# Attention and two expert layers in one kernel: weights read in 1 MB pieces, one subtraction on VectorE, zero rows written near head 12

## The chip, the cores and the metric

The kernel runs on one core of a Trainium2 chip. The metric is the time of one execution on the device in microseconds (us), the median of several runs. Engines are named as in the profile: PE is TensorE's matmul, PEld its loading of weights, DVE is VectorE, ACT ScalarE, POOL GpSimd and SP SyncE, which here issues nearly all DMA transfers.

## What is computed

Everything is float32. Cut to what matters:

```python
# q, k, v: 4 batches x 8 heads x 576 x 64; block-causal mask, blocks of 64
attn = softmax(q @ k.T / 8 + mask) @ v                 # 32 heads
x = attn.transpose(0, 2, 1, 3).reshape(2304, 512)
h = (x @ w1) * (x @ w2)                                # 512 -> 1024
x = (h @ w3) @ w_out                                   # 1024 -> 1024 -> 512
noisy = x @ w_gate + log1p(exp(x @ w_noise)) * noise   # 8 experts
top2, weights = two largest of noisy, softmax over the two
out[t] = sum over the two experts e: weight * (relu(x[t] @ e_w1[e]) @ e_w2[e])
```

## The kernel before

The work is staged in three. **Attention** goes over 32 heads. **MoE1** computes the dense expert and the router in nine chunks (`CH` = 256 tokens) and fills PE's gaps between heads. The **expert phase** (`phase3`) follows, eight experts on gathered rows. Two slots per token go into a table `idt` in DRAM, the rows themselves into `yt`.

Precision comes from pairs: a float32 value is split into a high part (a rounded copy, made by ACT) and a low part (value less high part), and `mm3` multiplies with three matmuls (lines 485 to 487). `split` (line 476 on ACT, line 480 on DVE) makes such a pair.

The dense weights `w1`, `w2`, `w3`, `w_out` lie in DRAM as 64-bit floats. They come in 40 pieces of 512 KB (`w_jobs`); `load64` (line 538) has SP load one into a tile `stg`, of which there are two; `conv64` (lines 547 to 549) makes float32 of it on DVE with three integer instructions, writing a tile `stf` (also two), and `split` then writes the pair into its resident tile `pc`. The load of piece n + 2 is issued behind the conversion of piece n, which sets its `stg` free. One call of `feed` does the `split` of the piece converted last and the conversion of the next. Some pieces may not be converted before a count of matmul units has been issued.

The order of the work is written out by hand in two strings of steps for each head, `FIRST` for heads up to 9 and `LATER` behind them: `s0`..`s3` are the scores of the next head (`s_unit`, lines 639 to 642) with their row maxima on DVE (line 653) and exponentials on ACT (line 658); `g0`..`g3` transpose the probabilities on PE (line 672) and copy them to `pt` (line 676); `a`, `b0`, `b1` multiply by v (lines 685, 697); `h` prepares the head after (`prep_h`, lines 607 to 612); `c` calls `feed`; `f2.9` asks for 2.9 us of fill. The fill is first 64 units (192 matmuls of 128x512) that fold `w3` and `w_out` into one matrix (`w_unit`), then MoE1's chunks: `ab` (lines 485 to 487, 128x256, three to a product) needs `w1` and `w2` pieces. A scheduler then orders each engine's queue by priorities; an engine works through its queue in order.

`prep_h` splits q and k: ACT makes both high parts `hi`, DVE the low part of q in place, POOL the low part of k, `kl` (line 612). POOL has little else to do among the first eight heads.

`setup` fills two small tiles `tr0`, `tr1`, and `setup_dram(0)` (lines 133 to 148) writes the empty-slot entries into `idt` (runs of 12, 8 and 512 bytes) and zeroes the last rows of `yt`, 0.8 MB. It is called at head 4 of the written order, and the scheduler puts it far ahead of that. The first slots are scattered into `idt` at 260.8 us.

## Time and profile before

| | |
|---|---|
| median of 3 runs | 1100.47 us (1100.3 to 1101.81) |
| profiled execution, its own time | 1103.1 us |
| its span, first to last instruction | 1101.2 us |
| mean granted clock of TensorE | 0.988 of full speed |
| busy over the span: PE, PEld | 1050.4 us, 941.2 us |
| busy over the span: DVE, ACT, POOL | 564.4 us, 494.9 us, 309.3 us |
| DMA | 136.34 MB, 124 GB/s in the mean |

The profile is of one execution on the chip. Busy time is the time in which an engine had at least one instruction at work; matmuls overlap, and their ends are modelled. A line such as "DVE stf L547 <- DMA stg" is read as: the instruction of line 547 that writes `stf` on DVE waited for the transfer into `stg`. The chain is the row of waits and work that ended last, followed backwards.

### The profile page before, as it was taken

Reading aid. Unit: us, or ns where it says so; the run is one execution under the profiler, and the core shown is the slowest. Engines: PE = TensorE matmul, PEld = TensorE weight load, DVE = VectorE, ACT = ScalarE, POOL = GpSimd, SP = SyncE. Lnnn points to the kernel's source line nnn. Section 1 sums busy time; section 2 is a strip of 40 time slices with the busy share of each in tenths; the row PEclk is TensorE's granted clock in tenths of the full one; section 3 lists DMA queues with packets and bytes.
Section 4 is the critical chain, followed back from the end, with each engine's and each line's share of the span. In section 5 each row is a group of like instructions: output and inputs, shape, how many; then the busy total and the mean of one; then the engine's idle time right before and its main releaser. Section 6 shows DMA issues by size and latency. Waiting matters only on the chain.

```text
span 1101.2 us, 17515 instructions
## 1 busy us (share of the span) xinstructions
PE 1050.4 (95%) x6588; PEld 941.2 (85%) x6588; DVE 564.4 (51%) x1270; ACT 494.9 (45%) x1180; POOL 309.3 (28%) x315
## 2 busy tenths in 40 slices
PE   4999978999999999999999999999999999999996
PEld 3767767799899999989999889889898989899885
DVE  5988889856665756532454453534333333434111
ACT  5765547666665656422223432433333333333111
POOL 3110122424252242422443325241413222120211
PEclk9999989999999999999999999999999999999999
DMA  9765775325634463322413556563545445351212
GB/s 218 237 199 193 196 200 180 123 79 132 196 96 105 143 156 121 107 68 59 77 40 87 126 106 184 173 163 96 148 102 144 107 125 125 106 115 30 39 20 32
DMA packets 80386, 136.34 MB, mean 124 GB/s; under 512 B 21437, under 2 KB 46757, under 8 KB 80293
## 3 DMA queue, kind: packets, MB, share of 16 engines
q1 hardware_dynamic: 70181, 113.98, 36.4%
q0 software_dynamic: 10112, 21.16, 10.7%
q8 instruction: 54, 0.88, 0.3%
q14 instruction: 39, 0.32, 0.1%
HBM read 103.92 MB, written 31.19 MB: 123 GB/s over the span
## 4 chain that ended last, share of the span: by engine, by line
PE 81%; DMA 8%; DVE 7%; ACT 1%; issue 1%; SPq 1%; POOL 0%; POOLq 0%; DVEq 0%; ACTq 0%
PE ph L485 13%; PE ph L486 13%; PE ph L487 13%; PE m L485 9%; PE m L486 9%; PE m L487 9%; DMA stg<-in_w_dram 4%; PE tp L672 4%; PE av L697 3%; PE sb L642 2%; PE sb L639 2%; PE m L939 1%; DVE stf L549 1%; DVE nm L653 1%; DMA stf<-in_m_dram 1%
## 5 line engine op out<-in xcount | busy, mean ns | idle before, releaser
L485 PE MATMUL m<-xh,pc 128*128 128x256 f32 x576 | 165.2, 290 | 5.6 <-DVE at L211 3.5
L486 PE MATMUL m<-xh,pc 128*128 128x256 f32 x576 | 163.1, 287 | 2.2 <-DVE xh L480 2.2
L487 PE MATMUL m<-xh,pc 128*128 128x256 f32 x576 | 161.2, 287 | 1.9 <-DVE pc L480 1.9
L485 PE MATMUL ph<-xt,pc 128*128 128x384 f32 (+1 forms) x512 | 156.0, 308 | 2.9 <-ACT xt L476 1.6
L486 PE MATMUL ph<-xt,pc 128*128 128x384 f32 (+1 forms) x512 | 157.0, 307 | 0.0
L487 PE MATMUL ph<-xt,pc 128*128 128x384 f32 (+1 forms) x512 | 156.9, 307 | 0.0
L954 DVE SCALAR_TENSOR_TENSOR ht<-ph,ht 128x384 fp32r<-128x384 f32 (+1 forms) x128 | 61.6, 489 | 148.7 <-ACT ht L953 143.5
L480 DVE TENSOR_TENSOR pc<-stf,pc 128x1024 fp32r<-128x1024 f32 (+1 forms) x92 | 92.3, 1016 | 87.2 <-ACT pc L476 83.8
L485 PE MATMUL ph<-pc,ht 128*128 128x512 f32 x320 | 127.8, 400 | 0.0
L486 PE MATMUL ph<-pc,ht 128*128 128x512 f32 x320 | 126.5, 396 | 0.0
L487 PE MATMUL ph<-pc,ht 128*128 128x512 f32 x320 | 126.4, 395 | 0.0
L981 POOL DMA_INDIRECT out_dram<-yo,ids x40 | 64.3, 1606 | 211.5 <-ACT yo L977 124.0
L485 PEld LDWEIGHTS m<-xh,pc 128*128 128x128 f32 x576 | 110.5, 193 | 7.2 <-DVE at L211 3.7
L953 ACT ACTIVATE ht<-ph 128x384 fp32r<-128x384 f32 (+1 forms) x128 | 55.0, 437 | 133.8 <-PE ph L487 127.1
L486 PEld LDWEIGHTS m<-xh,pc 128*128 128x128 f32 x576 | 110.3, 193 | 3.0 <-DVE xh L480 2.6
L487 PEld LDWEIGHTS m<-xh,pc 128*128 128x128 f32 x576 | 109.0, 192 | 2.7 <-DVE pc L480 2.4
L476 ACT CAST pc<-stf 128x1024 fp32r<-128x1024 f32 (+1 forms) x92 | 78.1, 864 | 73.8 <-DVE stf L549 32.5
L658 ACT ACTIVATE pb<-sb,nm 128x288 f32<-128x288 f32 (+3 forms) x192 | 93.5, 496 | 38.4 <-PE tp L672 17.3
L480 POOL TENSOR_TENSOR gt<-at,gt 128x256 fp32r<-128x256 f32 x72 | 57.2, 798 | 183.9 <-ACT gt L476 175.7
L485 PEld LDWEIGHTS ph<-xt,pc 128*128 128x128 f32 x512 | 95.7, 188 | 4.0 <-ACT xt L476 2.1
L612 POOL TENSOR_TENSOR kl<-qk,hi 128x576 fp32r<-128x576 f32 x32 | 47.5, 1484 | 177.2 <-ACT hi L610 136.6
L486 PEld LDWEIGHTS ph<-xt,pc 128*128 128x128 f32 x512 | 96.2, 188 | 0.6 <-DVE xt L480 0.2
(158 smaller groups left out, 2229.0 us busy)
## 6 DMA issues: line engine op xcount, KB each, us to landing
stf<-in_m_dram SPq DMA_DIRECT2D x52, 512.0 KB
...
```

The lines of the kernel that those rows point to most:

```text
L476: d = nc.scalar.copy(h, src)
L480: return d, eng.tensor_tensor(l, src, r32(h), op=OP.subtract)
L485: nc.tensor.matmul(out, a, c, start=first, stop=False)
L486: nc.tensor.matmul(out, a, d, start=False, stop=False)
L487: nc.tensor.matmul(out, b, c, start=False, stop=last)
L612: nc.gpsimd.tensor_tensor(c.kl, c.qk[:, 1, :], r32(c.hi[:, 1, :]), op=OP.subtract)
L658: nc.scalar.activation(pb[t][:, k0:k0 + src.free_size()], src, AF.Exp, bias=nm, scale=1.0, accum_out=sums[:, h // H, t + n, h % H:h % H + 1])
L672: nc.tensor.transpose(bank[:, n * P:(n + 1) * P], pb[t][:, kt * P:(kt + 1) * P], self.ident)
L697: nc.tensor.matmul(c.av[:, o0:o0 + w], c.vv[:, kt, :], c.pt[:, i, s0:s0 + w], start=(kt == 0 and i == 0), stop=(kt == 4 and i == m - 1))
L953: a = nc.scalar.activation(hh[:, 0, f, :], ph, AF.Relu)
L954: v = nc.vector.scalar_tensor_tensor(hh[:, 1, f, :], ph, 0.0, r32(hh[:, 0, f, :]), op0=OP.max, op1=OP.subtract)
L981: nc.gpsimd.indirect_dma_start(out=self.a["out"], out_offset=self.idx(e, i), in_=yo, in_offset=None, compute_op=OP.add)
```

## The change

- **Pieces.** `w_jobs` now gives 23 pieces for the same bytes: six of 512 KB among the first nine, and 17 of 1 MB. `stg` tiles are 8 KB a partition (two), `stf` is one tile of 4 KB instead of two of 2 KB. `moe1.conv` still counts half pieces.
- **Steps.** `FIRST` calls `feed` three times a head instead of five.
- **kl.** For heads 0 to 8 DVE makes `kl`, not POOL.
- **Table and zero rows.** `setup_dram(0)` is called at head 12, issued behind the store of head 11's result. `tr0` lies in one of the three `y` tiles until then.
- **Memory.** `pt` of heads 0 to 7 lies where `pt` of the later heads will; `stg` and `stf` get their own pool, closed at the last piece, and `yT` lies in a pool that opens then; tiles of the expert phase get padding and other names (not shown).

```diff
@@ -67,7 +67,7 @@
 
 
 
-FIRST = "g0 g1 t f2.9 c t c o g2 g3 t p s0 t t s1 s2 f2.9 c t a f2.9 t b0 t s3 h t t c c b1 v l"
+FIRST = "g0 g1 t f2.9 c t o g2 g3 t p s0 t t s1 s2 f2.9 c t a f2.9 t b0 t s3 h t t c b1 v l"
 LATER = "g0 g1 f2.6 o g2 p t c g3 t t t s0 s1 s2 t c t a f2.6 s3 b0 t t c f2.6 c t b1 h v l"
 
 
@@ -116,7 +117,7 @@
         self.wcat = p2.tile([P, 4, P], F32R, name="wcat")
         nc.scalar.copy(self.wcat, wg)
         nc.gpsimd.tensor_tensor(self.wcat[:, :, 16:32], wg[:, :, 0:16], r32(self.wcat[:, :, 0:16]), op=OP.subtract)
-        self.tr0 = self.px.tile([P, E, NSLOT], I32, name="tr0")
+        self.tr0 = p2.tile([P, 512], I32, name="y", bufs=3)[:, 0:E * NSLOT].rearrange("p (e s) -> p e s", e=E)
         nc.gpsimd.iota(self.tr0, pattern=[[0, E], [0, NSLOT]], base=NT, channel_multiplier=1)
         self.tr1 = p2.tile([NOV, P], I32, name="lt")
         nc.gpsimd.iota(self.tr1, pattern=[[1, P]], base=NT, channel_multiplier=0)
@@ -534,7 +535,8 @@
         return [(tab[:, b * P:e * P].rearrange("e (p i) -> p e i", p=P), ids[:, :, b:e]) for b, e in ((0, NA), (NA, NSLOT))]
 
     def load64(self, src, n):
-        t = self.stg.tile([P, 512], I64, name="stg")
+        w = n * src.shape[-1]
+        t = self.stg.tile([P, 1024], I64, name="stg", bufs=2)[:, 0:w]
         self.nc.sync.dma_start(t.rearrange("p (a b) -> p a b", a=n), src)
         return t
 
@@ -542,7 +544,7 @@
 
         v = self.nc.vector
         wi = t.bitcast(I32).rearrange("p (n w) -> p n w", w=2)
-        f = self.stg.tile([P, 512], F32, name="stf")
+        f = self.stg.tile([P, 1024], F32, name="stf")[:, 0:wi.shape[1]]
         fi = f.bitcast(I32)
         v.tensor_scalar(fi, wi[:, :, 1], 0x07FFFFFF, 3, op0=OP.bitwise_and, op1=OP.logical_shift_left)
         v.scalar_tensor_tensor(fi, wi[:, :, 1], -0x40000000, fi, op0=OP.bitwise_and, op1=OP.bitwise_or)
@@ -553,7 +555,8 @@
     def attention(self):
         tc, nc, a = self.tc, self.nc, self.a
         moe1 = self.moe1
-        with tc.tile_pool(name="p1", bufs=1, side="right") as p1, tc.tile_pool(name="stg", bufs=2, side="right") as self.stg, \
+        stgs = ExitStack()
+        with tc.tile_pool(name="p1", bufs=1, side="right") as p1, \
                 tc.tile_pool(name="psS", bufs=3, space=PSUM) as psS, \
                 tc.tile_pool(name="psT", bufs=2, space=PSUM) as psT, \
                 tc.tile_pool(name="psV", bufs=1, space=PSUM) as psV:
@@ -564,6 +567,8 @@
             nc.vector.tensor_copy(mkl, mk32[:, 0, :])
             nc.vector.tensor_copy(mkr, mk32[:, 1, 0:64])
             sums = p1.tile([P, B, 6, H], F32, name="sums")
+            pt0 = p1.tile([P, 2, PTW], F32, name="pt")
+            self.stg = stgs.enter_context(tc.tile_pool(name="stg", bufs=1, side="right"))
 
             hd = {}
             pxs = ExitStack()
@@ -609,7 +614,7 @@
                 nc.vector.scalar_tensor_tensor(lo, c.qk[64:128, 0, :], 0.125, r32(lo), op0=OP.mult, op1=OP.subtract)
                 nc.scalar.copy(c.hi[:, 1, :], c.qk[:, 1, :])
                 c.kl = buf(h, [P, S], F32R, "kl")
-                nc.gpsimd.tensor_tensor(c.kl, c.qk[:, 1, :], r32(c.hi[:, 1, :]), op=OP.subtract)
+                (nc.vector if h < NF - 1 else nc.gpsimd).tensor_tensor(c.kl, c.qk[:, 1, :], r32(c.hi[:, 1, :]), op=OP.subtract)
 
             def prep_v(h):
                 c = hd[h]
@@ -663,7 +668,7 @@
                 pb = pbs[h < H and h % 2]
                 if g == 0:
                     if h < H:
-                        c.pt = px.tile([P, 1, PTW], F32, name="pt", bufs=2)
+                        c.pt = pt0[:, h % 2:h % 2 + 1, :]
                     else:
                         c.pt = p1.tile([P, 2, PTW], F32R, name="pt")
                 base, skip, items = G_UNITS[g]
@@ -736,20 +741,24 @@
                 def wout(g):
                     return a["w_out"][:, g:g + 1, :], 1, g // 2, (g % 2) * 512, 0
 
-                def w3(ft, o):
-                    return a["w3"][ft, :, o:o + 512].unsqueeze(1), 1, 4 + ft % 2, o, 0 if ft < 2 else max(16, 8 * (ft - 1))
+                def wout2(g):
+                    return a["w_out"][:, g:g + 2, :], 2, g // 2, 0, 0
+
+                def w3(ft, o, w=512):
+                    return a["w3"][ft, :, o:o + w].unsqueeze(1), 1, 4 + ft % 2, o, 0 if ft < 2 else max(16, 8 * (ft - 1))
 
                 for half in range(2):
                     for ft in range(2):
                         yield w3(ft, half * 512)
-                    for g in range(4 * half, 4 * half + 4):
-                        yield wout(g)
+                    if half == 0:
+                        for g in range(2):
+                            yield wout(g)
+                    for g in range(2 + 2 * half, 4 + 4 * half, 2):
+                        yield wout2(g)
                 for ft in range(2, 8):
-                    for o in (0, 512):
-                        yield w3(ft, o)
+                    yield w3(ft, 0, 1024)
                 for m, (n, k, i) in enumerate(W12):
-                    for o in (0, 2):
-                        yield a[n][:, o:o + 2, k * 256:(k + 1) * 256], 2, i, o * 256, 0 if m < 2 else 64
+                    yield a[n][:, :, k * 256:(k + 1) * 256], 4, i, 0, 0 if m < 2 else 64
 
             jobs = list(w_jobs())
             raw = []
@@ -762,11 +771,12 @@
                     feed_half()
 
             def feed_half():
-                if len(conv) > moe1.conv:
-                    _, _, i, o, _ = jobs[moe1.conv]
-                    pc = self.pc[i]
-                    self.split((pc[:, 0, o:o + 512], pc[:, 1, o:o + 512]), conv[-1], low="dve")
-                    moe1.conv += 1
+                if len(conv) > wst.get("split", 0):
+                    _, _, i, o, _ = jobs[len(conv) - 1]
+                    pc, w = self.pc[i], conv[-1].shape[-1]
+                    self.split((pc[:, 0, o:o + w], pc[:, 1, o:o + w]), conv[-1], low="dve")
+                    wst["split"] = len(conv)
+                    moe1.conv += w // 512
                 n = len(conv)
                 if n < len(jobs) and wst.get("n", 0) >= jobs[n][4]:
                     conv.append(self.conv64(raw[n]))
@@ -847,8 +857,10 @@
                         sums_out((i - 1) // H if i > H else 0)
                     if i >= H:
                         moe1.ready = i // H
-                    if i == 4:
-                        moe1.setup_dram(0)
+                    if i == 12:
+                        assert not moe1.scat
+                        with tc.issue_after(self.x2w[i - 1].ins):
+                            moe1.setup_dram(0)
 
             for i in range(-1, BH):
                 if i == 2:
@@ -858,6 +870,9 @@
                 elif i == H:
                     pxs.close()
                     moe1.p2b = moe1.p2s.enter_context(tc.tile_pool(name="p2b", bufs=1, reuse_waits="tile"))
+                if i >= H and moe1.p2c is None and moe1.conv == 40:
+                    stgs.close()
+                    moe1.p2c = moe1.p2s.enter_context(tc.tile_pool(name="p2c", bufs=1, reuse_waits="tile"))
                 for op in (FIRST if i < NF else LATER).split():
                     step(i, i + 1, op)
             sums_out(B - 1)
```

What it moves on the engines, as built (file lines of the changed kernel are 1 to 16 higher):

SP's queue in the opening: `cst`, `fold`, `nz` are constants, `qk` a head's q and k, `v` and `vz` its v, `tr`, `lt` the table's filling, `yt<-cst` the zero rows. Before:

```order
L101 DMA fold<-in_cst_dram 32x16
L103 DMA nz<-in_noise_dram 128x144
L133 DMA idt<-tr_750 128x8x3
L593 DMA qk<-in_qk_dram 128x1152
L133 DMA idt<-tr_750 128x8x2
L538 DMA stg<-in_w_out_dram 128x512
L134 DMA idt<-lt 13x8x128
L602 DMA v<-in_v_dram 128x320
L538 DMA stg<-in_w_out_dram 128x512
L593 DMA qk<-in_qk_dram 128x1152
L146 DMA yt<-cst_577 128x3x8
L148 DMA yt<-cst_577 128x3x256 x2
```

With the change:

```order
L102 DMA fold<-in_cst_dram 32x16
L104 DMA nz<-in_noise_dram 128x144
L598 DMA qk<-in_qk_dram 128x1152
L607 DMA v<-in_v_dram 128x320
L540 DMA stg<-in_w_out_dram 128x512
L598 DMA qk<-in_qk_dram 128x1152
L540 DMA stg<-in_w_out_dram 128x512
L607 DMA v<-in_v_dram 128x320
L598 DMA qk<-in_qk_dram 128x1152
L540 DMA stg<-in_w_out_dram 128x1024
```

The three writes of `idt` and the three of `yt` are gone from here; the third `qk` load stands directly behind the constants.

SP's queue with the change near the store of head 11 (`x<-ev`, the row ahead of the first `idt`):

```order
L607 DMA v<-in_v_dram 128x320
L540 DMA stg<-in_w_dram 128x4x256 x2
L706 DMA x_61<-ev 128x576
L134 DMA idt<-y 128x8x3
L598 DMA qk<-in_qk_dram 128x1152
L134 DMA idt<-y 128x8x2
L135 DMA idt<-lt 13x8x128
L147 DMA yt<-cst_501 128x3x8
L149 DMA yt<-cst_501 128x3x256 x2
L607 DMA v<-in_v_dram 128x320
L706 DMA x_61<-ev 128x576
```

The last two weight loads stand ahead of the six writes, and one `qk` load between them.

DVE's queue near head 4, where `nm` are row maxima. Before:

```order
L548 SCALAR_TENSOR_TENSOR stf<-stg,stf 128x512
L653 TENSOR_REDUCE nm_988<-sb 128x1
L547 TENSOR_SCALAR stf<-stg 128x512
L549 SCALAR_TENSOR_TENSOR stf<-stg,stf 128x512
L548 SCALAR_TENSOR_TENSOR stf<-stg,stf 128x512
L653 TENSOR_REDUCE nm_996<-sb 128x1
L549 SCALAR_TENSOR_TENSOR stf<-stg,stf 128x512
L653 TENSOR_REDUCE nm_1003<-sb 128x1
L653 TENSOR_REDUCE nm_1056<-sb 128x1
L480 TENSOR_TENSOR pc_70<-stf,pc_70 128x512 x2
```

With the change:

```order
L658 TENSOR_REDUCE nm_871<-sb 128x1
L549 TENSOR_SCALAR stf<-stg 128x1024
L658 TENSOR_REDUCE nm_878<-sb 128x1
L658 TENSOR_REDUCE nm_935<-sb 128x1
L550 SCALAR_TENSOR_TENSOR stf<-stg,stf 128x1024
L551 SCALAR_TENSOR_TENSOR stf<-stg,stf 128x1024
L658 TENSOR_REDUCE nm_935<-sb 128x1
L481 TENSOR_TENSOR pc_70<-stf,pc_70 128x1024
```

Before, two half pieces are converted in turn, and other work stands between the last instruction of a conversion (L549) and the low part (L480), which waits for ACT. With one `stf`, the low part (L481) must come before the next conversion. Counted over the whole order: before, every piece has at least two DVE instructions between the two; with the change, 3 of 23 have none (one of 512 columns, two of 1024), and 3 have one short one.

PE, counted in its order up to the last `av` matmul of a head: of the 192 matmuls of `w_unit` 30, 69, 103 and 148 stood before the end of heads 3, 5, 6 and 7; now 24, 50, 90 and 151; all 192 by the end of head 8 in both. Of MoE1's first matmuls 75, 107, 135, 167 and 191 stood before the end of heads 9 to 13; now 71, 95, 119, 143 and 191 (counted from behind head 8).

## Rows read from the trace of the kernel before

**Rows 1.** Stretches: length; busy us of PE, PEld, DVE, ACT, POOL; PEclk, DMA share, GB/s.
```profile
core 0: us, PE busy (x) PEld busy (x) DVE busy (x) ACT busy (x) POOL busy (x), PEclk, DMA share, GB/s
0.00:31.70 31.70, 17.49 (x74) 13.20 (x75) 19.65 (x40) 16.74 (x41) 10.10 (x26) 1.00 0.99 240
31.70:121.30 89.60, 85.46 (x456) 64.86 (x455) 80.00 (x155) 60.02 (x163) 9.67 (x7) 0.98 0.62 197
121.30:215.30 94.00, 77.89 (x489) 68.46 (x488) 82.66 (x154) 56.03 (x152) 25.17 (x20) 0.91 0.60 172
215.30:660.00 444.70, 441.03 (x3106) 408.27 (x3105) 240.28 (x716) 215.81 (x582) 155.33 (x157) 1.00 0.42 108
```

**Rows 2.** Timeline of PE beside its busy times: starts of neighbouring matmuls, and one idle gap.
```profile
155.41 0.38 PE L485 MATMUL m<-xh,pc 128*128 128x256 f32 x1 [3.46 <-DVE at L211]
155.75 0.28 PE L487 MATMUL m<-xh,pc 128*128 128x256 f32 x1
155.87 0.28 PE L485 MATMUL m<-xh,pc 128*128 128x256 f32 x1
```

**Rows 3.** The chain that ended last: shares in 31.7 to 121.3 us, and pieces.
```profile
by line: DMA stg<-in_w_dram 31.7%; DMA stg<-in_w_out_dram 10.2%; DVE stf L549 7.0%; PE av L697 5.8%; DVE stf L548 5.6%; PE tp L672 5.3%; DVE stf L547 4.2%; PE m L486 4.2%; PE m L485 4.1%; issue 4.1%; PE m L487 3.9%; DVE hi L609 3.4%; PE sb 
90.74 5.84 DMA stg<-in_w_dram
...
145.02 9.55 DMA stg<-in_w_dram
```

**Rows 4.** Waits from 0 to 215.3 us: who <- for whom: us, times, longest; then L547 with its idle time.
```profile
ACT pc L476 <- DVE stf L549: 32.5, 20, 5.1
...
L547 DVE TENSOR_SCALAR stf<-stg 128x512 int32<-128x512 int32 x40 | 20.6, 515 | 17.7 <-DMA stg<-in_w_dram 14.9 <-DMA stg<-in_w_out_dram 2.7
```

**Rows 5.** Stretches of 2 us in the opening, columns as in rows 1.
```profile
4.00:6.00 2.00, 0.00 (x0) 0.00 (x0) 0.00 (x0) 0.00 (x0) 0.00 (x0) 1.00 1.00 363
12.00:14.00 2.00, 0.63 (x2) 0.63 (x3) 2.00 (x5) 1.93 (x7) 1.37 (x1) 1.00 1.01 59
14.00:16.00 2.00, 1.79 (x8) 1.25 (x6) 1.97 (x3) 1.27 (x3) 1.01 (x3) 1.00 0.83 46
```

**Rows 6.** Timeline of the opening: qk loads on SP, their first readers on ACT, PE's gap.
```profile
1.64 0.43 SPq L593 DMA_DIRECT2D qk<-in_qk_dram  x1
6.28 0.68 ACT L607 ACTIVATE hi<-qk 128x576 fp32r<-128x576 f32 x1 [4.25 <-DMA qk<-in_qk_dram]
11.37 0.51 SPq L593 DMA_DIRECT2D qk<-in_qk_dram  x1
19.66 0.68 ACT L607 ACTIVATE hi<-qk 128x576 fp32r<-128x576 f32 x1 [3.17 <-DMA qk<-in_qk_dram]
21.45 0.69 PE L672 MATMUL tp<-ident,pb 128*128 128x128 f32 x2 [3.23 <-ACT pb L658]
```

**Rows 7.** Groups on DVE, then ACT: first 512 columns wide early, then 1024 columns late.
```profile
L480 DVE TENSOR_TENSOR pc<-stf,pc 128x512 fp32r<-128x512 f32 x22 | 14.9, 679 | 0.3 <-ACT pc L476 0.2
...
L480 DVE TENSOR_TENSOR pc<-stf,pc 128x1024 fp32r<-128x1024 f32 x40 | 48.1, 1223 | 76.7 <-ACT pc L476 74.2 <-PE ph L487 2.6
...
L476 ACT CAST pc<-stf 128x512 fp32r<-128x512 f32 x40 | 25.0, 625 | 33.2 <-DVE stf L549 32.5 <-PE m L486 0.6
...
L476 ACT CAST pc<-stf 128x1024 fp32r<-128x1024 f32 x40 | 40.9, 1048 | 30.3 <-DMA stf<-in_m_dram 23.9 <-PE ph L487 6.4
```

**Rows 8.** Timeline: kl on POOL, the DVE instruction beside it; the last of seven such.
```profile
7.61 1.41 POOL L612 TENSOR_TENSOR kl<-qk,hi 128x576 fp32r<-128x576 f32 x1 [4.36 <-ACT hi L610]
7.78 1.52 DVE L547 TENSOR_SCALAR stf<-stg 128x512 int32<-128x512 int32 x1
...
72.17 1.54 DVE L547 TENSOR_SCALAR stf<-stg 128x512 int32<-128x512 int32 x1
```

**Rows 9.** Timeline near head 12: a qk load on SP and the kl that needs it.
```profile
202.34 0.34 SPq L593 DMA_DIRECT2D qk<-in_qk_dram  x1
214.00 1.44 POOL L612 TENSOR_TENSOR kl<-qk,hi 128x576 fp32r<-128x576 f32 x1 [6.67 <-ACT hi L610]
```

8 lines of the change are left out of this document (5 added, 3 removed).

## Prediction

> **What bounds the kernel now.** I first cut the span into stretches [rows 1]. From 215.3 us on PE is busy all the time (441.0 of 444.7 us in the fourth row), so whatever comes earlier there shortens the end by as much; the change leaves the number of matmuls as it is. All that it can win or lose lies before 215.3 us, that is in the opening (0 to 31.7 us, to the store of head 0), stretch B (31.7 to 121.3 us, heads 1 to 7) and stretch C (121.3 to 215.3 us, heads 8 to 13).
>
> In B PE looks full too, 85.5 of 89.6 us. The timeline says otherwise [rows 2]: matmuls start 0.12 us apart and each is booked with 0.28 us, so one busy microsecond of PE can hold less than half as much work as it could. What is nearly full is DVE: 80.0 of 89.6 us in B, 82.7 of 94.0 in C [rows 1]. The chain through B confirms it [rows 3]: 42% of it is transfers into `stg` and 17% the three instructions that convert them. So here weights are brought in and converted, and DVE and the loads take turns in holding it up. Of DVE's idle time up to 215.3 us, 17.7 us is spent before L547 on such loads, and ACT's casts stand for 32.5 us behind L549 [rows 4]. ACT works in order, so the exponentials behind a cast stand there too. In C the price shows on PE: a piece issued at 145.02 us lands after 9.55 us [rows 3], DVE stands before its L547 with the product `at` queued behind, and PE stands for 3.46 us on that `at` [rows 2].
>
> The opening is short of DMA. At 4 to 6 us the transfers run at 363 GB/s; at 12 to 16 us, with `idt`'s writes in the queue, at 59 and 46 GB/s, though the DMA engines count as busy [rows 5].
>
> **The change part by part**, against the profiled execution's 1103.1 us (its span is 1101.2 us).
>
> *Opening.* SP issues six writes fewer between the loads; on DMA go the runs of 12 and 8 bytes and 0.8 MB of zeros. Head 0's `qk` took 4.64 us from issue (1.64) to first reader (6.28); the third `qk`, with the `idt` writes around it, took 8.29 us (11.37 to 19.66). Behind it ACT's exponentials stood, and PE for 3.23 us [rows 6]. The difference, 3.65 us, covers that gap; I take **-3.2 us**, bounds 0 and -3.65 (plus whatever the next loads win, which lies in the load waits below).
>
> *Wide pieces.* 17 pairs of half pieces become one piece each, so DVE runs four instructions less for each pair. The low part costs 679 ns at 512 columns and 1223 ns at 1024 [rows 7]: one wide instead of two saves 0.135 us. No row has the other three at 1024 columns; two of them also read two operands from SBUF and run at much the same rate, so I take the same saving: 17 x 4 x 0.135 = **-9.2 us** of DVE. Bounds: -2.3 (the low part alone) and -9.2. ACT saves 2 x 625 - 1048 = 202 ns a pair, 3.4 us in all, which I count at nothing: ACT has about a third of its time free [rows 1].
>
> *kl on DVE.* Nine times 0.75 us (679 ns plus 64 columns at (1223 - 679)/512 ns each) [rows 7] is +6.7 us. Against it: while POOL makes `kl`, the DVE instruction beside it stands still. L547 takes 515 ns in the mean [rows 4] and 1.52 and 1.54 us beside a `kl` [rows 8]; seven of the nine `kl` hit one in this way, about 1.0 us each, -7.0 us. Together **-0.3 us**. The bounds are -7.0 (DVE makes it in idle time) and +6.7 (POOL's hits fall on other work). `kl` is ready sooner (0.75 instead of 1.41 us), which I count at nothing.
>
> *Load waits.* Two 1 MB tiles stand for twice as much work of DVE. A half piece takes 5.84 us where it holds the chain [rows 3]; at the 363 GB/s of [rows 5] the further 512 KB are 1.4 us, so a wide one takes about 7.3 us, an estimate. Against it DVE has two wide pieces, 2 x 4.4 us (1223 ns three times, about 0.7 once), plus the heads' own work; before it had 2 x 2.5 us against 5.84. Loads that stand alone are then covered; those in a crowd, as the 9.55 us one, are not, and a wide one in a crowd takes longer. I take half of the 17.7 us, **-8.8 us**, bounds 0 and -17.7.
>
> *One stf.* The low part now ends a piece before the next begins, and waits for ACT's cast, 625 or 1048 ns [rows 7]. In the order three pieces have nothing in between (2.7 us in all) and three have one instruction of some 0.3 to 0.45 us (2.0 us): **+4.7 us**. Bounds: 0 (ACT and DVE drift apart) and +21.6 (every one of 17 x 1.048 and 6 x 0.625 is waited for).
>
> *Fewer steps.* PE's order holds 24 matmuls less by the end of head 12, at 0.12 us [rows 2] **+2.9 us** if PE can't use the time otherwise; the lag of 19 by head 5 is made up by head 7 and I count it at nothing (bound +4.4 at twice 0.12 us each).
>
> *Writes at head 12.* The last weight loads are issued ahead of them. What could suffer is the `qk` load between them; before, such a load had 11.7 us from issue (202.34) to its `kl` (214.00) [rows 9], and needs 4.64 us alone. The clog of [rows 5], some 4 us, fits: **0**, and +4 if that slack is gone. The scatter at 260.8 us and the `y` and `lt` tiles that are held until then come later still. `pt`'s common place costs nothing: PE does a head's `av` before the next head's transposes anyway.
>
> Sum: -3.2 - 9.2 - 0.3 - 8.8 + 4.7 + 2.9 = **-13.9 us**. PE has room for it: it stands 4.1 us in B, 16.1 us in C [rows 1], and more than that inside its busy time. The profile would then show 1103.1 - 13.9 = 1089.2 us. The median of the runs lies 2.6 us below the profiled execution (1100.47 against 1103.1), so **1086.6 us**. C's granted clock of 0.91 (in the mean of its 2.4 and 1.2 GHz) against 1.00 behind it I leave out of the sum; if PE stands less, it is gain on top.
>
> **The rivals.** A measurement can tell about 0.2% from no change, 2.2 us here.
>
> - *The loads vanish altogether.* All of the 17.7 us goes and the lag costs nothing: -3.2 - 9.2 - 0.3 - 17.7 + 4.7 = -25.7, 1074.8 us. For it: no wait on `stg` is long but the crowded one. Against it: x, `qk` and weight loads still meet in C. The Trainium skill (DMA: Bandwidth & Descriptors, Bandwidth) gives 6.15 us for a transfer of 1 MB issued by GpSimd; by it, an estimate, a wide piece would always be covered and the time would be this rival's. No row here has such a load, and it says nothing of a crowd.
> - *The opening alone.* Heads in B are held by the round trip of scores, maxima, exponentials and transposes, not by DVE's total, and what DVE wins turns into idle time: 1103.1 - 3.2 - 2.6 = 1097.3 us. For it: DVE has 9.6 us idle in B already. Against it: the chain runs through the conversion.
> - *One stf makes it slower.* DVE waits for ACT at every piece, because ACT has exponentials ahead of the cast: +21.6 in place of +4.7, and since DVE is then late the loads win nothing: -3.2 - 9.2 - 0.3 + 21.6 = +8.9, 1109.4 us. It decides from a mean wait of 12.7 / 23 = 0.55 us a piece. For it: maxima, which feed the exponentials, stand behind the waiting low part. Against it: before, ACT waits for DVE at the cast, not DVE for ACT [rows 4].
>
> **How the numbers follow.** Forecast (some 1081 to 1093 us): 0.50. Loads vanish (below 1081): 0.15. Opening alone (1093 to 1098.3): 0.20. No difference (1098.3 to 1102.7): 0.05. Slower: 0.10. So faster 0.85, same 0.05, slower 0.10. The range of 8 in 10 reaches from 1075 us, where half of the first rival is left out, to 1101 us, which leaves out the slower case and a little more.
>
> **What would show it.** In the profile after: the third `qk` read about 4 to 5 us after its issue and no gap of PE near 18 to 21 us; 17 `stf` instructions of 1024 columns near 1.2 us; no DVE instruction stretched to 1.5 us beside a `kl` before head 8; idle time before the first conversion instruction at 9 us or so; idle time of DVE before the low part at some 5 us; the store of head 13, now at 215.3 us, near 201 us, and the same length from there to the end. The prediction is wrong if the heads of B come no faster, if DVE's wait on ACT's cast passes 12 us, or if PE shows new gaps behind head 13.

## The result, and the profile after

The changed kernel takes **1085.29 us** (median of 4 runs, 1083.17 to 1086.11) against 1101.0 us for the kernel before beside it: a ratio of **0.9852**, 95% interval 0.9839 to 0.9865. The forecast was 1086.6 us. The profiled execution's span is 1083.8 us, 17.4 us shorter.

First the stretches, cut at the same stores of head results as [rows 1] (heads 0, 7 and 13) and at the first reading of the finished table `idt`. Of before, the last stretch, which [rows 1] lacks; columns as there:

```profile
660.00:1101.00 441.00, 428.56 (x2472) 386.38 (x2470) 141.78 (x209) 146.33 (x246) 108.98 (x107) 0.99 0.44 107
```

And of the changed kernel:

```profile
0.00:29.20 29.20, 18.70 (x86) 14.65 (x86) 21.81 (x46) 18.61 (x49) 5.65 (x22) 1.00 0.84 268
29.20:110.00 80.80, 79.34 (x441) 62.50 (x441) 73.42 (x118) 57.14 (x145) 1.87 (x1) 1.00 0.63 208
110.00:202.90 92.90, 79.15 (x488) 69.56 (x487) 83.11 (x124) 54.75 (x143) 28.77 (x21) 0.89 0.70 180
202.90:646.50 443.60, 440.54 (x3107) 408.55 (x3106) 243.37 (x716) 218.17 (x583) 156.23 (x156) 1.00 0.40 108
646.50:1083.80 437.30, 423.71 (x2473) 386.58 (x2471) 142.19 (x209) 146.52 (x246) 110.28 (x107) 0.99 0.44 108
```

The opening is 2.5 us shorter, stretch B 8.8, stretch C only 1.1, the long middle 1.1 and the expert phase 3.7. In B DVE has 8% less to do (73.4 us, before 80.0) and PE fills 79.3 of 80.8 us. C hardly changed: DVE is as busy as before (83.1 against 82.7 us), and PE's mean clock is lower (0.89 against 0.91). The last line was not forecast at all: the same number of matmuls (2473 and 2472 records) takes PE 4.85 us less.

Starts of the stores of a head's result on SP, in us:

| head | 0 | 3 | 5 | 7 | 8 | 11 | 12 | 13 | 31 |
|---|---|---|---|---|---|---|---|---|---|
| before | 31.7 | 60.3 | 89.8 | 121.3 | 141.7 | 186.5 | 206.1 | 215.3 | 464.4 |
| after | 29.2 | 52.8 | 73.4 | 110.0 | 129.6 | 170.9 | 187.3 | 202.9 | 461.6 |

By head 5 the lead is 16.4 us, at head 7 11.3, at head 8 12.1, at head 12 18.7, at head 13 12.4. (Heads run ahead or behind as fill is put between them, so a lead counts where the fill done is the same: at head 8, when all 192 of `w_unit` are in, and at head 13.)

DVE's groups up to 215 us (line, operation, shapes, count | busy us, mean ns | idle before, releaser), which answer to [rows 4, 7, 8]:

```profile
L550 DVE SCALAR_TENSOR_TENSOR stf<-stg,stf 128x1024 int32<-128x1024 int32 x17 | 24.6, 1450 | 0.3
L551 DVE SCALAR_TENSOR_TENSOR stf<-stg,stf 128x1024 int32<-128x1024 int32 x17 | 21.6, 1270 | 0.2
L481 DVE TENSOR_TENSOR pc<-stf,pc 128x1024 fp32r<-128x1024 f32 x17 | 21.5, 1264 | 3.5 <-ACT pc L477 3.4
...
L549 DVE TENSOR_SCALAR stf<-stg 128x1024 int32<-128x1024 int32 x17 | 12.8, 755 | 0.2
L617 DVE TENSOR_TENSOR kl<-qk,hi 128x576 fp32r<-128x576 f32 x9 | 6.8, 755 | 0.2
```

and the waits of the same stretch (who <- for whom: us, times, longest):

```profile
ACT pc L477 <- DVE stf L551: 15.2, 10, 4.6
...
DVE pc L481 <- ACT pc L477: 4.3, 7, 1.1
```

The first conversion instruction, now L549, never waits for a load: the 17.7 us of [rows 4] are 0.2 us of idle time that no load ends. With the six pieces of 512 columns (15.0 us) the conversions and low parts are booked with 95.5 us on DVE instead of 111.4. (These are durations; neighbouring instructions overlap in the trace, so the engine's busy time fell by less, as the part on the prediction shows.) ACT waits 15.2 us behind a conversion, before 32.5.

### The profile page after: what moved, and what is told of

Read it like the earlier page. It is cut to its first block, busy times and chain, and to the rows that moved or that the text cites. A ratio compares the mean times of both kernels' runs of the same rounds, so it can differ in the third digit from the quotient of the medians.

```text
span 1083.8 us, 17396 instructions
## 1 busy us (share of the span) xinstructions
PE 1041.4 (96%) x6588; PEld 941.8 (87%) x6588; DVE 563.9 (52%) x1211; ACT 495.2 (46%) x1163; POOL 302.8 (28%) x306
## 4 chain that ended last, share of the span: by engine, by line
PE 78%; DVE 3%; DMA 2%; ACT 1%; issue 1%; SPq 0%; POOL 0%; POOLq 0%; ACTq 0%; DVEq 0%
PE ph L486 13%; PE ph L488 13%; PE ph L487 13%; PE m L486 9%; PE m L487 9%; PE m L488 9%; PE tp L677 3%; PE av L702 3%; PE sb L647 1%; PE sb L644 1%; PE m L955 1%; DMA stf<-in_m_dram 1%; DMA yt<-cst 1%; PE m L244 1%; DVE pc L481 1%; PE m L235 1%
## 5 line engine op out<-in xcount | busy, mean ns | idle before, releaser
L481 DVE TENSOR_TENSOR pc<-stf,pc 128x1024 fp32r<-128x1024 f32 (+1 forms) x75 | 88.1, 1190 | 87.9 <-ACT pc L477 83.8
L486 PE MATMUL ph<-pc,ht 128*128 128x512 f32 x320 | 126.0, 395 | 0.0
L488 PE MATMUL ph<-pc,ht 128*128 128x512 f32 x320 | 124.6, 390 | 0.0
L487 PE MATMUL ph<-pc,ht 128*128 128x512 f32 x320 | 124.5, 390 | 0.0
L481 POOL TENSOR_TENSOR gt<-at,gt 128x256 fp32r<-128x256 f32 x72 | 59.2, 826 | 187.2 <-ACT gt L477 168.9
L663 ACT ACTIVATE pb<-sb,nm 128x320 f32<-128x320 f32 (+3 forms) x192 | 93.7, 498 | 23.3 <-PE tp L677 15.5
L486 PEld LDWEIGHTS ph<-xt,pc 128*128 128x128 f32 x512 | 95.8, 188 | 4.5 <-DVE ht L970 2.1
L477 ACT CAST pc<-stf 128x1024 fp32r<-128x1024 f32 (+1 forms) x75 | 74.8, 1016 | 54.0 <-DMA stf<-in_m_dram 32.8
L487 PEld LDWEIGHTS ph<-xt,pc 128*128 128x128 f32 x512 | 96.1, 188 | 0.5 <-DVE xt L481 0.2
L488 PEld LDWEIGHTS ph<-xt,pc 128*128 128x128 f32 x512 | 96.2, 188 | 0.0
```

Source lines behind the costliest of these rows:

```text
L477: d = nc.scalar.copy(h, src)
L481: return d, eng.tensor_tensor(l, src, r32(h), op=OP.subtract)
L486: nc.tensor.matmul(out, a, c, start=first, stop=False)
L487: nc.tensor.matmul(out, a, d, start=False, stop=False)
L488: nc.tensor.matmul(out, b, c, start=False, stop=last)
L663: nc.scalar.activation(pb[t][:, k0:k0 + src.free_size()], src, AF.Exp, bias=nm, scale=1.0, accum_out=sums[:, h // H, t + n, h % H:h % H + 1])
```

## The experiments

"Ratio" is the time over that of the kernel before, run on the same chip, with its 95% interval. Most kernels are the changed one with one edit, so their distance from 0.9852 is what the edit does, together with the order that the scheduler makes of it; "alone" means an edit of the kernel before. In the traces the order on PE, DVE, ACT and POOL is the same, instruction by instruction, within three groups: the kernel before and the one with the placement alone; the change, the change without the placement and the two with the writes at head 13 and nothing else in the attention part but padding; and the two with `kl` on DVE up to head 13. Between these groups, and in every other kernel, it differs.

### The placement of tiles, alone and taken away

In `trans` the tiles `xt1` and `wv` of the expert phase were padded or renamed; the matrix tiles `ht0` and `ht1` behind them moved from byte addresses 198560 and 140224 in a partition to 198528 and 140672.

```diff
-        x = self.xt[e, s] = (self.pa if s == 0 else self.pb).tile([P, 2, 4, n * P], F32R, name=f"xt{s}")
-        wv = self.wv[e, s] = self.pa.tile([P, n], F32, name=f"wv{s}", bufs=2)
+        x = (self.pa if s == 0 else self.pb).tile([P, 8 * n * P + 112 * s], F32R, name=f"xt{s}")
+        x = self.xt[e, s] = x[:, 0:8 * n * P].rearrange("p (m d c) -> p m d c", m=2, d=4)
+        wv = self.wv[e, s] = self.pa.tile([P, n], F32, name=f"wv{s}{e % 2}")
```

The kernel before with this alone:

> The kernel before with only the padding of xt1 and the other names of wv, which move the tiles ht0 and ht1 (the stationary side of the expert phase's 960 matmuls of 128x512) from bytes 198560 and 140224 of a partition to 198528 and 140672, both whole multiples of 128. Theory (the place of the stationary tile sets the pace): those matmuls start 0.227 us apart instead of 0.233, 960 x 0.0065 = 6.2 us less, 1094 to 1096 us. Rival (the changed kernel's faster expert phase comes from what ran before it): no difference, 1099 to 1102 us and 0.233 us apart.

Measured: 1097.61 us, ratio 0.9962 (0.9943 to 0.9982), between the two ranges and faster than the kernel before. Its order is that of the kernel before, yet in its profile head 13 is stored at 211.4 us (before 215.3): stages of single profiled executions can differ by some 4 us without any edit there. The changed kernel without it:

> The changed kernel without that padding and those names. Theory: the matmuls of 128x512 in the expert phase are back at 0.233 us apart and 4 to 6 us are lost against the changed kernel, 1089 to 1092 us; what is left against the kernel before is what the attention part won. Rival: as the changed kernel, 1084 to 1087 us.

Measured: 1090.97 us, 0.9895 (0.9875 to 0.9916), so 4.7 us of the gain (0.0043 of 1101) are gone. The timeline of PE in the expert phase (start, duration) shows where. Before:

```profile
735.19 0.40 PE L487 MATMUL ph<-pc,ht 128*128 128x512 f32 x1
735.42 0.40 PE L485 MATMUL ph<-pc,ht 128*128 128x512 f32 x1
735.66 0.39 PE L486 MATMUL ph<-pc,ht 128*128 128x512 f32 x1
735.89 0.40 PE L487 MATMUL ph<-pc,ht 128*128 128x512 f32 x1
```

With the placement alone:

```profile
735.26 0.39 PE L486 MATMUL ph<-pc,ht 128*128 128x512 f32 x1
735.49 0.39 PE L487 MATMUL ph<-pc,ht 128*128 128x512 f32 x1
735.71 0.39 PE L485 MATMUL ph<-pc,ht 128*128 128x512 f32 x1
735.94 0.39 PE L486 MATMUL ph<-pc,ht 128*128 128x512 f32 x1
```

Three matmuls take 0.70 us there and 0.68 here. Over all 916 pairs of neighbours the starts are 233.4 and 227.4 ns apart in the mean, and 960 times the difference of 6.0 ns make 5.7 us. The mean is 227.4 ns in all ten kernels with the placement and 233.4 in all four without it. From the store of head 13 to the end the placement takes the kernel before from 885.9 to 880.8 us, and without it the change goes from 880.9 to 886.9. The gain in the medians, 4.2 and 4.7 us, is a little lower, within its interval.

### Table and zero rows back among the first heads

```diff
-                    if i == 12:
-                        assert not moe1.scat
-                        with tc.issue_after(self.x2w[i - 1].ins):
-                            moe1.setup_dram(0)
+                    if i == 4:
+                        moe1.setup_dram(0)
```

> The changed kernel with the table's filling and the zero rows called at head 4 again. By the prediction's step (3.2 us won in the opening, nothing lost at head 12) it is slower than the changed kernel by 3 us, 1087.5 to 1089.5 us. Theory now, from the trace after (10 us of a zero-row write on the chain near head 12, PE idle for 3 us there): the opening wins 3 us and head 12 gives back as much or more, so this one is between 2 us faster and 1 us slower than the changed kernel, 1083 to 1086.5 us.

Measured: 1089.89 us, 0.9887 (0.9864 to 0.9909): 3.9 us slower than the change, with intervals that just touch. The prediction's step (-3.2 us) holds in size, the theory read from the trace after does not. Two stretches of the opening, first of this kernel, then of the change, show the clog of [rows 5] again, at 36 against 305 GB/s:

```profile
16.00:18.00 2.00, 1.21 (x7) 0.97 (x6) 1.92 (x6) 1.88 (x7) 0.00 (x0) 1.00 0.61 36
```

```profile
16.00:18.00 2.00, 0.62 (x5) 0.38 (x4) 1.92 (x6) 2.00 (x8) 1.25 (x1) 1.00 0.92 305
```

The store of head 0 comes at 31.97 us (29.18 with the change), that of head 3 at 59.70 (52.82); in between DVE stands once for 6.1 us on a half piece of `w_out`, where the change does not wait for loads at all. In exchange head 12 takes 13.3 us here and 16.5 with the change.

### The same writes one head later

```diff
-                    if i == 12:
+                    if i == 13:
```

> The changed kernel with the six writes one head later, behind the store of head 12, when the last weight loads have landed. Theory (the writes at head 12 delay the last two weight loads and a qk load): the wait on the chain goes and 2 to 5 us are won against the changed kernel, 1080 to 1083.5 us. Rival (the writes are covered, as predicted): no difference, 1084 to 1087 us.

Measured: 1083.89 us, 0.9836 (0.9814 to 0.9857), by the ratios 1.8 us better than the change, within the intervals, so not shown by this run alone. Head 12 takes 13.2 us, and head 13, which has the writes now, 15.9 (15.6 with the change). What the writes do at head 12 with the change stands in the timeline of SP:

```profile
173.55 0.66 SPq L134 DMA_DIRECT2D idt<-y  x1
174.26 2.65 SPq L135 DMA_DIRECT2D idt<-lt  x1
176.95 0.46 SPq L147 DMA_DIRECT2D yt<-cst  x1
177.46 2.79 SPq L149 DMA_DIRECT2D yt<-cst  x2
180.35 0.97 SPq L607 DMA_DIRECT2D v<-in_v_dram  x1
```

in stretches of 2 us (columns as above):

```profile
178.00:180.00 2.00, 2.00 (x14) 2.00 (x14) 1.69 (x3) 0.38 (x1) 0.00 (x0) 0.72 0.92 83
180.00:182.00 2.00, 2.00 (x17) 1.91 (x16) 1.02 (x3) 1.24 (x4) 0.00 (x0) 1.00 1.41 120
182.00:184.00 2.00, 1.65 (x11) 1.12 (x9) 2.00 (x4) 2.00 (x9) 0.00 (x0) 1.00 0.94 70
...
186.00:188.00 2.00, 0.00 (x0) 0.00 (x0) 1.97 (x2) 1.30 (x2) 2.00 (x2) 1.00 0.72 176
```

and in the chain:

```profile
177.99 9.96 DMA yt<-cst
```

The transfers run at 70 to 120 GB/s with the engines booked full, the chain passes through the zero rows for 9.96 us, and PE stands for the two microseconds at 186. So the writes were not free at head 12.

### kl back on POOL, kl on DVE for longer, and kl alone

```diff
-                (nc.vector if h < NF - 1 else nc.gpsimd).tensor_tensor(c.kl, ...
+                nc.gpsimd.tensor_tensor(c.kl, ...
```

> The changed kernel with kl on POOL for all heads. By the prediction's step (6.7 us of DVE against 7 us of stretched DVE instructions) no difference, 1084.5 to 1087.5 us, with DVE instructions of 1.4 us and more beside the kl of heads 0 to 8. Rival (kl is also ready sooner on DVE, and its stall falls on wide instructions): 1088 to 1091 us.

Measured: 1093.46 us, 0.9918 (0.9904 to 0.9932): 7.3 us slower than the change, beyond the rival's range too. DVE's low part of q (line 614) and POOL's `kl` become ready almost together, and collide. Two rows of this kernel's DVE timeline, the first behind a `kl` that began at 65.40 and ended at 67.28, the second with none beside it until its last 0.1 us:

```profile
66.23 1.67 DVE L614 SCALAR_TENSOR_TENSOR hi<-qk,hi 64x576 fp32r<-64x576 f32 x1
...
103.05 0.76 DVE L614 SCALAR_TENSOR_TENSOR hi<-qk,hi 64x576 fp32r<-64x576 f32 x1
```

The Trainium skill (SBUF — State Buffer, Who interferes with whom) has VectorE and GpSimd share one pair of ports under an exclusive lock, for a VectorE operation with two inputs in SBUF against a GpSimd one that reads SBUF. The rows agree, at 1.67 against 0.76 us, and where DVE was first (a low part from 37.19 us), POOL took 2.01 us instead of 1.44:

```profile
37.22 2.01 POOL L617 TENSOR_TENSOR kl<-qk,hi 128x576 fp32r<-128x576 f32 x1 [8.61 <-ACT hi L615]
...
76.47 1.44 POOL L617 TENSOR_TENSOR kl<-qk,hi 128x576 fp32r<-128x576 f32 x1 [9.19 <-ACT hi L615]
```

Yet the collisions are not the loss: up to 127 us the stretched instructions cost DVE about 7 us (L614 3.9, the pieces of 512 columns 3.2), as much as nine `kl` cost it with the change (6.8). At the store of head 8, when these `kl` are done and all 192 `w_unit` matmuls are in, this kernel is not behind (128.9 us, the change 129.6). The balance of the prediction is right for the heads that it is about; the loss comes behind them, where `kl` is on POOL in both kernels. What differs there is the order that the scheduler made (48 of MoE1's matmuls by the end of head 9, with the change 72) and a crowd: in this kernel's chain a load of `v`, 160 KB, takes

```profile
138.91 10.66 DMA v<-in_v_dram
```

with ACT's `vv` waiting 6.2 us for it and DVE's low part 5.3 us for the cast behind `vv`. How the 7.3 us divide between order and crowd stays open.

Now the other way, more of them on DVE:

```diff
-                (nc.vector if h < NF - 1 else nc.gpsimd).tensor_tensor(c.kl, ...
+                (nc.vector if h < 14 else nc.gpsimd).tensor_tensor(c.kl, ...
```

> The changed kernel with kl on DVE up to head 13 instead of head 8. Near heads 9 to 13 POOL also makes xab, vv and gt, and five kl there stretch a DVE instruction by 1 us each. Theory (as for heads 0 to 8, a trade of 0.75 us for 1.0 us): within 2 us of the changed kernel, 1083 to 1087 us. Rival (DVE is the bound there and the stalls come from the other POOL work anyway): slower by the full 5 x 0.75 us, 1088 to 1091 us.

Measured: 1083.4 us, 0.9833 (0.9817 to 0.985), 2.1 us better than the change by the ratios, though the intervals overlap. The order changed as well (48, 96 and 144 of MoE1's matmuls by heads 9, 10 and 11, with the change 72, 96 and 120), so this is not `kl` alone. Last, `kl` of heads 0 to 8 on DVE in the kernel before, alone:

```diff
-                nc.gpsimd.tensor_tensor(c.kl, ...
+                (nc.vector if h < NF - 1 else nc.gpsimd).tensor_tensor(c.kl, ...
```

> The kernel before with one edit: kl of heads 0 to 8 on DVE. By the prediction's step (-0.3 us) no difference, 1100 to 1102 us. If kl on POOL costs what taking it back cost in the changed kernel (7 us), 1093 to 1096 us. If DVE simply carries more work, up to 1108 us.

Measured: 1114.4 us, 1.0107 (1.0086 to 1.0129): **11.8 us slower**, outside all three. Its DVE groups show that the three integer instructions and the low part became shorter (30.2 + 28.5 + 28.0 + 18.9 = 105.6 us, before 111.4), and that the wait on loads grew from 17.7 to 22.7 us:

```profile
L547 DVE TENSOR_SCALAR stf<-stg 128x512 int32<-128x512 int32 x40 | 18.9, 474 | 22.7 <-DMA stg<-in_w_dram 18.0 <-DMA stg<-in_w_out_dram 4.6
```

### The writes alone

The kernel before, with `tr0` in a `y` tile, as in the change, and

```diff
-                    if i == 4:
-                        moe1.setup_dram(0)
+                    if i == 12:
+                        assert not moe1.scat
+                        with tc.issue_after(self.x2w[i - 1].ins):
+                            moe1.setup_dram(0)
```

> The kernel before with one edit: the table's filling and the zero rows at head 12, tr0 in a y tile. By the prediction's steps (-3.2 us for the opening, 0 at head 12) 1097 to 1099 us. If the writes cost 2 to 3 us at head 12, as the trace of the change reads, 1099 to 1102 us. If the opening also speeds up the loads of heads 1 to 7, below 1096 us.

Measured: 1107.85 us, 1.005 (1.0033 to 1.0066): 5.5 us **slower**. The opening gains more than forecast (the store of head 0 at 27.2 us, before 31.7). Head 1 (41.5, before 41.0) and head 7 (124.7, before 121.3) come later, but with more fill done: 24 `w_unit` matmuls instead of 12 by head 1, 170 instead of 148 by head 7. At the store of head 8, with 192 in both, this kernel is 1.2 us ahead (140.5, before 141.7), though DVE stands on loads for 17.1 us, as before. So most of the 5.5 us are lost behind that; where is shown at the end of the next part.

### Half pieces again

The change, but with 40 pieces of 512 KB and five `feed` a head; one `stf`. (The diff is cut: the pieces of `w_out`, `w1` and `w2` are halved in the same way.)

```diff
-FIRST = "... c t o g2 ... t t c b1 v l"
+FIRST = "... c t c o g2 ... t t c c b1 v l"
...
-                    yield w3(ft, 0, 1024)
+                    for o in (0, 512):
+                        yield w3(ft, o)
```

> The changed kernel with the 40 half pieces and five feed steps a head in FIRST, everything else as changed (two stg tiles, one stf, kl on DVE, writes at head 12). By the prediction's steps: DVE runs 9 us more, the load waits of some 17 us come back, the one stf costs as before: 1096 to 1106 us. Rival (the early heads were held by their own round trip, the pieces add little): 1086 to 1091 us.

Measured: 1109.06 us, 1.0065 (1.0051 to 1.0079), beyond the end that was given. The heads come sooner than in any other kernel (head 13 stored at 181.0 us), because PE has less to do between them, and it stands later: 52.6 busy of the 60 us from 210 on, with the change 60.0. Matmuls that stand ahead of the end of a head in PE's order, counted from its start:

```
                w_unit by head 6, 8, 9     MoE1 by head 9, 10, 11, 13
before              103, 192, 192              76, 108, 136, 192
the change           90, 192, 192              72,  96, 120, 192
one stf, halves      66, 156, 180               0,  12,  36,  72
two stf, halves     124, 192, 192              48, 136, 172, 216
kl alone            125, 192, 192              48, 136, 172, 216
writes alone        124, 192, 192              48, 136, 172, 216
```

With one `stf` and narrow pieces the scheduler put conversions, and the matmuls that need them, far back: 20 half pieces are converted by the store of head 7 and 31 by that of head 13 (27 and 40 with two `stf`, in the run below). At this pace DVE never waits for a load, though the pieces are just as narrow: in these two kernels narrow pieces make it stand only where conversions follow each other faster. A further kernel has two `stf` of 512 columns (and `stg` tiles of 512) and is otherwise the same:

```diff
-        f = self.stg.tile([P, 1024], F32, name="stf")[:, 0:wi.shape[1]]
+        f = self.stg.tile([P, 512], F32, name="stf", bufs=2)[:, 0:wi.shape[1]]
```

> The change with 40 half pieces and five feeds a head, as in the earlier run, but with two stf tiles as before the change. Theory: with one stf the conversions, and with them the w_unit and MoE1 matmuls, are put far back in PE's order (72 of MoE1's matmuls by the end of head 13 instead of 192), and it is this, not the narrowness of the pieces, that cost the earlier run 20 us; then 1087 to 1094 us (the kernel before, less 4 for the placement, 3 for the opening and 1 to 7 for kl). Rival, narrow pieces cost DVE and the loads 15 us or more whatever the tiles: 1098 us or more.

Measured: 1103.08 us, 1.0013 (0.9998 to 1.0028): the time of before, though `kl`, the writes and the placement are those of the change. The theory is half right: the fill is early again and 5.7 us (0.0052 of 1102) are back with it, but **17.7 us** (1.0013 less 0.9852) come with the width of the pieces. They are not all waits on loads, for the order is not that of the change (see the table). Its DVE row against the change's:

```profile
L549 DVE TENSOR_SCALAR stf<-stg 128x512 int32<-128x512 int32 x40 | 18.9, 474 | 19.8 <-DMA stg<-in_w_dram 15.4 <-DMA stg<-in_w_out_dram 4.2
```

and its chain from 100 to 160 us, by line:

```profile
by line: DMA stg<-in_w_dram 42.3%; DVE stf L551 9.4%; DVE stf L550 6.8%; DMA xab<-x 6.6%; DVE stf L549 6.6%; issue 6.2%; DVE pc L481 4.6%; DVE nm L658 3.4%; DVE pt L683 3.0%; DVE xr L194 2.0%; SPq L168 2.0%; SPq L173 2.0%; DVE hi L614 1.9%;
```

The wait on loads is 19.8 us with halves and none with wide pieces, in kernels that do the same work in another order. Where the 17.7 us lie can be read at two places. At the store of head 8 all 192 `w_unit` matmuls and at most one of MoE1's are in, in each of these kernels:

| | before | the change | kl back on POOL | two stf, halves | kl alone | writes alone |
|---|---|---|---|---|---|---|
| store of head 8, us | 141.7 | 129.6 | 128.9 | 141.7 | 149.1 | 140.5 |

Two kernels of the same order, the change with and without the placement, differ here by 1.1 us. With halves the same work stands 12.1 us later. The second place is far behind the weights, whose last piece is converted at 204 us or sooner in all of these kernels: 360 to 480 us, first the change, then two `stf` with halves, `kl` alone and the writes alone:

```profile
360.00:480.00 120.00, 118.31 (x879) 110.81 (x878) 71.34 (x216) 65.80 (x186) 43.66 (x43) 1.00 0.38 112
360.00:480.00 120.00, 112.40 (x792) 104.14 (x791) 73.55 (x187) 67.58 (x196) 42.66 (x40) 0.96 0.45 117
360.00:480.00 120.00, 113.61 (x807) 105.33 (x806) 75.53 (x199) 68.31 (x198) 42.96 (x40) 0.97 0.46 126
360.00:480.00 120.00, 113.30 (x813) 104.45 (x812) 74.61 (x194) 70.30 (x203) 43.56 (x40) 0.98 0.46 121
```

In the kernel before PE is busy there for 118.2 us at a clock of 1.00, with the change for 118.3; the three kernels, whose fill counts agree, lose 4.6 to 5.9 us of it, at a lower clock. No dense weight is loaded any more, so this part is not a wait on those loads. The order of the fill is what these three have in common and the two others have not; that it is the cause was not shown. So some 12 us of the 17.7 come up to head 8, where weights are loaded and converted, and some 6 lie far behind.

### A version that beats both

Writes at head 13 and `kl` on DVE up to head 13 together:

```diff
-                (nc.vector if h < NF - 1 else nc.gpsimd).tensor_tensor(c.kl, ...
+                (nc.vector if h < 14 else nc.gpsimd).tensor_tensor(c.kl, ...
...
-                    if i == 12:
+                    if i == 13:
```

> The change with its two weak places mended together: table and zero rows written behind the store of head 12, one head later, and kl on DVE up to head 13. If the gains of the two alone (about 1.5 us by the ratios to the kernel before, and 2 us) add up, 1080 to 1082 us. If both remove the same wait in heads 9 to 13, no more than either alone, 1083 to 1084 us.

Measured: **1078.68 us**, 0.9794 (0.9782 to 0.9807), 6.4 us better than the change. That is more than the two gains added (1.8 + 2.1), but within their intervals. Against the kernel with `kl` on DVE up to head 13, whose order it has, the writes at head 13 bring 4.3 us (0.9794 against 0.9833, intervals apart), so at head 12 they do cost time. The stretches from 150 to 210 us, of the change and then of this kernel:

```profile
150.00:180.00 30.00, 25.02 (x155) 22.54 (x156) 28.56 (x47) 18.40 (x48) 7.41 (x6) 0.83 0.70 197
180.00:210.00 30.00, 26.31 (x166) 22.84 (x165) 24.32 (x37) 19.23 (x51) 12.51 (x9) 0.94 0.54 119
```

```profile
150.00:180.00 30.00, 26.10 (x182) 22.12 (x182) 29.81 (x49) 22.59 (x64) 8.87 (x7) 1.00 0.57 176
180.00:210.00 30.00, 28.45 (x181) 24.51 (x180) 18.97 (x35) 16.84 (x47) 7.70 (x7) 1.00 0.63 113
```

PE's clock is granted in full in both (0.83 and 0.94 with the change), and 363 matmul records stand where the change has 321 (the order of the fill differs too). Its head 13 is stored at 195.3 us. Another kernel, with the writes at head 13 and the tiles `hi`, `pb` and `vv` of the later heads put at multiples of 128 bytes as well, showed nothing more than the writes at head 13 without that:

```diff
-                c.vv = p1.tile([P, 5, P], F32R, name="vv")
+                c.vv = p1.tile([P, 5 * P + 24], F32R, name="vv")[:, 0:5 * P].rearrange("p (a b) -> p a b", a=5)
...
-                    nm = p1.tile([P, 3], F32, name=f"nm{t}")
+                    nm = p1.tile([P, 27 if t == 4 else 3], F32, name=f"nm{t}")[:, 0:3]
```

> The kernel with the writes at head 13 and, on top, hi, pb and vv of the heads from 8 on placed at whole multiples of 128 bytes (96 bytes of padding behind nm4 and behind vv). If a stationary tile's place costs 6.5 ns a matmul everywhere, 24 heads x (12 scores + 10 av) x 6.5 ns = 3.4 us are won against the kernel with the writes at head 13: 1078 to 1081.5 us. Rival (only the long matmuls of the expert phase show it, where PE does nothing else): no difference, 1082 to 1085 us.

Measured: 1081.87 us, 0.9833 (0.9814 to 0.9853), against 0.9836 without.

## Why the prediction came out, point by point

The total was right (1086.6 forecast, 1085.29 measured), and most of the gain came where it was forecast, ahead of head 13, from loads and conversions. That the number is so close is partly luck: two terms of DVE were mis-sized, and a gain of 4.7 us that the sum did not hold came in behind head 13. Step by step:

- **Opening, -3.2:** the store of head 0 comes 2.5 us sooner. The third `qk` is read 4.2 us after its issue (10.79 to 14.98), as forecast; of PE's gap before the transposes (3.23 us) 1.38 is left:

```profile
10.79 0.35 SPq L598 DMA_DIRECT2D qk<-in_qk_dram  x1
...
14.98 0.69 ACT L612 ACTIVATE hi<-qk 128x576 fp32r<-128x576 f32 x1 [0.56 <-DMA qk<-in_qk_dram]
...
17.65 0.69 PE L677 MATMUL tp<-ident,pb 128*128 128x128 f32 x2 [1.38 <-ACT pb L663]
```

- **Wide pieces, -9.2:** mis-sized. The durations did shrink as forecast (with `kl` on DVE in both, 105.9 us with halves and two `stf`, 95.5 with the change), but neighbours overlap, and the 0.135 us that a wide instruction saves in duration is mostly overlap. Of the kernel before, then of the change:

```profile
63.83 0.68 DVE L549 SCALAR_TENSOR_TENSOR stf<-stg,stf 128x512 int32<-128x512 int32 x1
64.43 0.68 DVE L548 SCALAR_TENSOR_TENSOR stf<-stg,stf 128x512 int32<-128x512 int32 x1
...
65.62 1.23 DVE L550 SCALAR_TENSOR_TENSOR stf<-stg,stf 128x1024 int32<-128x1024 int32 x1
66.76 0.69 DVE L481 TENSOR_TENSOR pc<-m,pc 128x512 fp32r<-128x512 f32 x1
```

  From start to start 512 columns take 0.60 us and 1024 take 1.14, so a wide one saves 0.06 us here, and 17 x 4 of them 4.1 us, an estimate. DVE's whole busy time up to the store of head 13 agrees: 183.0 us with halves and two `stf`, 178.3 with the change, 4.7 less:

```profile
0.00:224.23 224.23, 191.62 (x1091) 156.31 (x1092) 183.00 (x359) 135.53 (x358) 33.65 (x45) 0.95 0.63 186
```

- **kl on DVE, -0.3:** as a balance of DVE about right (nine `kl` +6.8, conversions 111.4 to 105.6, so -5.8). With wide pieces it holds as a time too where it applies: at head 8 the kernel with `kl` on POOL is 0.7 us ahead. The 7.3 us that it loses behind, and the 11.8 us that `kl` costs alone, came with new orders of the work, which the step did not reckon with (that they are the cause was not shown).
- **Load waits, -8.8:** mis-sized. "I take half of the 17.7 us": all of it went. But DVE's idle time up to head 13 fell only by 8.4 us (33.0 to 24.6); the rest came back as waits for PE, ACT and POOL, the cast of the next item among them. That 8.4 is near 8.8 is luck. Even the crowded load that held C [rows 2, 3] no longer does: the change's chain from 110 to 203 us has no load of weights among its nine longest pieces.
- **One stf, +4.7:** 4.3 us in 7 waits, the longest 1.1. The rival in which it makes the kernel slower did not come with wide pieces; with halves it did (1109.06 us), by PE's order, not by DVE's waits on the cast (5.3 us there).
- **Fewer steps, +2.9, and the lag of `w_unit` at nothing:** the lag seems to have been paid. By head 5, 19 matmuls were owed, 4.4 us at 0.23 us each, the bound that was given, and the lead fell from 16.4 us at head 5 to 11.3 at head 7, by when 22 had been made up, with PE busy for 79.3 of 80.8 us in B. No run has the lag alone.
- **Writes at head 12, 0:** wrong, they cost there. Moved one head on, head 12 takes 3.2 us less; 1.8 us of it reach the end with the change's order (within the intervals) and 4.3 us with that of `kl` on DVE up to head 13.
- **Memory and padding, left out of the sum:** wrong, -4.2 us alone and -4.7 as the change has it. The words "the same length from there to the end" failed with it: from the store of head 13 it was 885.9 us and is 880.9.

So the sum came out by errors that offset one another. The 12.4 us at head 13 can be read on DVE: its busy time up to there fell by 4.0 us (19.65 + 80.00 + 82.66 in [rows 1], 21.81 + 73.42 + 83.11 now) and its idle time by 8.4; 13.9 had been forecast. Behind head 13 came 5.0 us that had not. Both are differences of single executions, with the spread of some 4 us named above. The loads did vanish, as in the rival "the loads vanish altogether" (1074.8 us), and the time did not follow it: the wide pieces gave half of what it reckons with, and other waits took the place of those on loads. Some of that lies in C, in the clog of the writes and in POOL's work there (`kl`, `vv`, `gt`, `xab`). DVE's groups from 127 to 215 us:

```profile
L550 DVE SCALAR_TENSOR_TENSOR stf<-stg,stf 128x1024 int32<-128x1024 int32 x6 | 10.1, 1682 | 0.1
...
L614 DVE SCALAR_TENSOR_TENSOR hi<-qk,hi 64x576 fp32r<-64x576 f32 x6 | 7.9, 1308 | 0.8 <-ACT hi L612 0.6
L549 DVE TENSOR_SCALAR stf<-stg 128x1024 int32<-128x1024 int32 x6 | 5.3, 880 | 0.1
```

Undisturbed they take 1220, 756 and 687 ns: six of each are stretched by 7.2 us in all. With `kl` on DVE up to head 13 the same groups take 1310, 937 and 685 ns, so 5.6 us of the stretching are gone; what they save in time is not separated from the order. By the Trainium skill's 1 MB in 6.15 us (DMA: Bandwidth & Descriptors, Bandwidth), for transfers that GpSimd issues, a wide piece would, as an estimate, always have been covered. No load is timed by itself here; that DVE never waits for a load with the change agrees. The "opening alone" rival falls with stretch B, which it left as it was and which is 8.8 us shorter.

Taken away one at a time from the change, placement, writes, `kl` and width cost 4.7, 3.9, 7.3 and 17.7 us, 33.6 together, twice the 16.3 that all of them gave. `kl` and the writes cost time when they were put in alone. In the kernel before and in the three kernels of half pieces with two `stf` DVE stands on loads for 17.1 to 22.7 us, and each edit also makes the scheduler write another order: the last three rows of the table, three different edits, agree in their counts, with less fill by head 9 and more by head 10 than before, and DVE's orders still differ. In 120 to 150 us these keep PE busy for 20.5 to 22.7 us of 30 at a mean clock of 0.74 to 0.81, before for 25.99 at 0.89.

The store of head 8 and the stretch from 360 to 480 us tell much of the 5.5 and 11.8 us. The writes alone are 1.2 us ahead of the kernel before at head 8 and lose 4.9 us of PE between 360 and 480 us; `kl` alone is 7.4 us behind at head 8 (3.6 of it in the opening, head 0 at 35.3 us) and loses 4.6 there. So close to 5 us of each loss lie where no weights are loaded. The three can also be set against each other, as their fill is alike: from the writes alone to two `stf` with halves, `kl`, the placement and the rest of the memory come in, for 4.1 us, which the placement alone gives (4.2), so `kl` brought nothing there; from `kl` alone to it the writes come in instead, for 10.4 us, some 6 beyond the placement. The intervals leave some 3 us to each, but neither edit shows a cost there, where the fill is alike, of the size that it had alone. That the new order is the cause, and how it loses the time, was not shown.
